# One listed order for every engine, one PSUM pool of eight banks, and denominators in PSUM, in a three-layer kernel

## The chip, the cores and the metric

The kernel runs on one core of one Trainium2 chip. The metric is the device time of one launch in microseconds; the median of the runs is compared. Engines go by their names in the profile: PE is TensorE, PEld its weight loads, DVE VectorE, ACT ScalarE, POOL GpSimd, and SP the queue that issues every transfer of this kernel.

## What is computed

The program is a gated linear recurrence (an mLSTM), followed by two MLPs on its outputs.

```python
for t in range(S):                                  # B, H, S, D = 2, 8, 768, 40
    m_new = np.maximum(f_gate[:, :, t] + m, i_gate[:, :, t])
    f_stab = np.exp(f_gate[:, :, t] + m - m_new)
    i_stab = np.exp(i_gate[:, :, t] - m_new)
    C = f_stab * C + i_stab * outer(vt, kt)         # state, 40 x 40 per head
    n = f_stab * n + i_stab * kt
    denom = np.maximum(np.abs(n . qt), 1.0)
    y[:, :, t] = sigmoid(o_gate[:, :, t]) * (C @ qt) / denom
x = y, as 1536 tokens x 320
x = ((x @ w_a) * (x @ w_b)) @ w_out                 # d_ff = 1536
g = x @ w_in                                        # d_ff = 2048
return (g * sigmoid(g)) @ w_out2
```

## The kernel before

**Units.** The recurrence is computed in chunks of 128 steps. A unit u is one chunk of one batch (12 units; u's chunk is u // 2). `load_q`, `load_k`, `load_kvo` and `load_fs` fetch a unit's data. `scores` makes q k products (`s_u`), `weigh` multiplies them by the decay matrix `e_u`, which `decays` makes on VectorE, `values` multiplies by v (`y_u`, from L360), `carried` adds what the state brings (`y_u`, from L370), `update` and `advance` make the next state. `combine` and `outputs` give the unit's x, and `x_transposed` turns it and splits it into a high and a low part in `xring`. Units 0 and 1 have no state before them; their decays come from `factors` (`fb_u`), those of later units from a table in DRAM (`fsd`).

**First MLP.** Its 12 weight blocks of 128 hidden columns arrive as 64-bit numbers. `split_w1` narrows each one on ScalarE and VectorE and splits it into a high and a low part (ScalarE copies, GpSimd subtracts at L195). The tail rows are moved to other partitions by a transfer (`w_j` from `tl_j`). `PASSES` cuts the work into passes: a block of 2 or 3 units against 5, 3, 4 or all 12 weight blocks. In a pass, a step `m3.5.a` is the first product of pass 3 with weight block 5, `.b` the second one with the multiply (L526) and the split of g, `.c` the second layer into accumulators, and `.end` writes x1, with one evicting instruction for all columns and one more for the 64 tail columns. The pass products are TensorE line 479, the second layer lines 488 to 490.

**Second MLP.** It goes in three blocks of 4 units against 16 weight blocks, in a loop behind the list (`prep2`, `block`, `slots`).

**What sets the order.** The steps are written down in `ORDER`, and a scheduler places each instruction on its engine from there: steps with `!` get a higher priority, `AFTER` holds back three steps, and 150 warm-up matmuls (`warm`) have the lowest priority of all, so that they fill gaps. The second MLP is not in the list. SP issues transfers in the order that the scheduler gives. PSUM has three pools: 3 banks of accumulators, 2 for first-layer products (and the scores of units 0 to 3), 3 for everything else of the recurrence.

**Denominators.** In `outputs` VectorE makes max(-y, y) (L426), max with 1 (L428) and the reciprocal (L429) in SBUF, multiplies (L431) and copies the last 64 columns of x once more behind it (L434), for the transposes.

## Time and profile before

| | |
|---|---|
| median of 3 runs | 492.58 us (492.13 to 498.36) |
| span of the profiled execution | 524.2 us |
| that execution's own time around the span | not on the page |
| TensorE busy in it | 506.7 us (97%) |
| VectorE, ScalarE, GpSimd busy | 197.0, 206.7, 254.8 us |
| mean granted clock of TensorE | 0.828 |

Durations of single instructions come from the one profiled execution. A busy time of TensorE counts matmuls that overlap and modelled ends, so it tells when the engine has something in it and not how fast it goes. The granted clock is a share of 2.4 GHz; the profile shows two values here, 0.85 and 0.50 (1.2 GHz), and a stretch's value is the mean of them.

### The profile page before, as it was taken

Reading aid. Unit: us, or ns where it says so; the run is one execution under the profiler, and the core shown is the slowest. Engines: PE = TensorE matmul, PEld = TensorE weight load, DVE = VectorE, ACT = ScalarE, POOL = GpSimd, SP = SyncE. Lnnn points to the kernel's source line nnn. Section 1 sums busy time; section 2 is a strip of 40 time slices with the busy share of each in tenths; the row PEclk is TensorE's granted clock in tenths of the full one; section 3 lists DMA queues with packets and bytes.
Section 4 is the critical chain, followed back from the end, with each engine's and each line's share of the span. In section 5 each row is a group of like instructions: output and inputs, shape, how many; then the busy total and the mean of one; then the engine's idle time right before and its main releaser. Section 6 shows DMA issues by size and latency. Waiting matters only on the chain.

```text
span 524.2 us, 8077 instructions
## 1 busy us (share of the span) xinstructions
PE 506.7 (97%) x3133; PEld 478.7 (91%) x3133; DVE 197.0 (38%) x328; ACT 206.7 (39%) x447; POOL 254.8 (49%) x289
## 2 busy tenths in 40 slices
PE   7999989699999999999999999999999999999996
PEld 6999879699999999999999999888888888889885
DVE  7677988968433345423731545300000000000000
ACT  4235665553222321212744545833334332342322
POOL 5429897896532241313753687843332233232331
PEclk9576887868888888888888888888888888888888
DMA  6475875734310011301450344000001000010001
GB/s 231 155 226 159 257 218 170 242 98 113 92 57 1 1 60 61 94 1 55 135 197 1 111 157 137 38 1 1 1 0 51 0 1 1 0 51 0 2 0 50
DMA packets 25089, 42.30 MB, mean 81 GB/s; under 512 B 2156, under 2 KB 18348, under 8 KB 25052
## 3 DMA queue, kind: packets, MB, share of 16 engines
q1 hardware_dynamic: 25052, 41.80, 25.5%
q8 instruction: 24, 0.39, 0.3%
q14 instruction: 13, 0.11, 0.1%
HBM read 38.99 MB, written 2.02 MB: 78 GB/s over the span
## 4 chain that ended last, share of the span: by engine, by line
PE 79%; POOL 8%; DVE 4%; ACT 4%; DMA 2%; issue 2%; SPq 0%; ACTq 0%; POOLq 0%; DVEq 0%
PE h L479 38%; PE acc L488 9%; PE acc L489 9%; PE acc L490 9%; POOL w_j L195 5%; PE s_u L347 5%; PE y_u L360 3%; PE warm L298 2%; ACT cvt_j L188 2%; PE px_u L458 1%; POOL g L195 1%; PE y_u L370 1%; DVE e_u L327 1%; PE fb_u L318 1%; POOL tl_j L195 1%
## 5 line engine op out<-in xcount | busy, mean ns | idle before, releaser
L479 PE MATMUL h<-xring,w_j 128*128 128x256 f32 (+2 forms) x1088 | 202.6, 333 | 3.5 <-DVE g L526 2.5
L479 PEld LDWEIGHTS h<-xring,w_j 128*128 128x128 f32 x1088 | 174.0, 198 | 9.9 <-DVE g L526 3.3
L195 POOL TENSOR_TENSOR g2w<-gw,g2w 128x512 fp32r<-128x512 f32 x48 | 61.7, 1287 | 117.6 <-ACT g2w L499 117.6
L195 POOL TENSOR_TENSOR g<-g,g 128x256 fp32r<-128x256 f32 (+1 forms) x60 | 54.7, 911 | 92.0 <-ACT g L499 91.8
L195 POOL TENSOR_TENSOR w_j<-cvt_j,w_j 128x320 fp32r<-128x320 f32 (+2 forms) x72 | 68.7, 955 | 6.6 <-ACT w_j L223 3.0
L479 PE MATMUL h<-xeven,w_j 128*128 128x512 f32 x256 | 71.0, 417 | 0.2 <-ACT gw L531 0.2
L531 ACT ACTIVATE gw<-h 128x512 f32<-128x512 f32 x48 | 28.8, 600 | 87.4 <-PE h L479 84.0
L488 PE MATMUL acc<-w_j,g2w 128*128 128x320 f32 x192 | 61.1, 324 | 0.0
L489 PE MATMUL acc<-w_j,g2w 128*128 128x320 f32 x192 | 60.9, 323 | 0.0
L479 PEld LDWEIGHTS h<-xeven,w_j 128*128 128x128 f32 x256 | 48.1, 192 | 11.6 <-ACT gw L531 0.5
L499 ACT CAST g<-g 128x256 fp32r<-128x256 f32 (+1 forms) x60 | 26.8, 447 | 71.7 <-DVE g L526 71.6
L526 DVE TENSOR_TENSOR g<-a,h 128x256 f32<-128x256 f32 (+1 forms) x60 | 28.1, 469 | 65.0 <-PE h L479 58.5
L488 PE MATMUL acc<-w_j,g 128*128 128x320 f32 x144 | 47.1, 331 | 0.0
L489 PE MATMUL acc<-w_j,g 128*128 128x320 f32 x144 | 46.1, 324 | 0.0
L520 ACT ACTIVATE a<-h 128x256 f32<-128x256 f32 (+1 forms) x60 | 25.6, 426 | 50.4 <-PE h L479 50.4
L190 DVE SCALAR_TENSOR_TENSOR cvt_j<-raw_j,cvt_j 128x704 uint32<-128x704 uint32 (+2 forms) x40 | 42.9, 1074 | 0.9
L490 PE MATMUL acc<-w_j,g2w 128*128 128x320 f32 x192 | 41.3, 323 | 0.0
L499 ACT CAST g2w<-gw 128x512 fp32r<-128x512 f32 x48 | 29.8, 621 | 28.0 <-PE acc L490 27.2
L488 PEld LDWEIGHTS acc<-w_j,g2w 128*128 128x128 f32 x192 | 36.9, 192 | 2.4
L489 PEld LDWEIGHTS acc<-w_j,g2w 128*128 128x128 f32 x192 | 36.7, 191 | 2.4
L188 ACT ACTIVATE cvt_j<-raw_j 128x704 f32<-128x704 f32 (+2 forms) x40 | 28.8, 724 | 23.4 <-POOL w_j L195 21.3
L490 PE MATMUL acc<-w_j,g 128*128 128x320 f32 x144 | 36.5, 328 | 0.7 <-POOL g L195 0.7
(95 smaller groups left out, 642.3 us busy)
## 6 DMA issues: line engine op xcount, KB each, us to landing
raw_j<-in_w_dram SPq DMA_DIRECT2D x16, 704.0 KB, 5.4
raw_j<-in_w_dram SPq DMA_DIRECT2D x12, 512.0 KB
kvo_u<-in_kvo_dram SPq DMA_DIRECT2D x12, 480.0 KB, 3.8
raw_j<-in_w_dram SPq DMA_DIRECT2D x12, 448.0 KB, 5.1
e_u<-fsd SPq DMA_DIRECT2D x10, 512.0 KB
qT_u<-in_q_cols_dram SPq DMA_DIRECT2D x12, 180.0 KB, 3.1
kz<-in_k_cols_dram SPq DMA_DIRECT2D x36, 60.0 KB
out_dram<-osb SPq DMA_DIRECT2D x12, 160.0 KB, 1.8
```

Source lines behind the costliest of these rows:

```text
L188: nc.scalar.activation(out=c, in_=hi32.bitcast(F32), func=ACT.Prelu, scale=2.0 ** -111, alpha=-2.0 ** 32)
L190: nc.vector.scalar_tensor_tensor(out=cu, in0=lo32, scalar=29, in1=cu, op0=ALU.logical_shift_right, op1=ALU.bitwise_or)
L195: return eng.tensor_tensor(out=out_, in0=x, in1=hi.bitcast(F32), op=ALU.subtract)
L347: nc.tensor.matmul(out=s[:, i], lhsT=kz[u % 2][:, j, g], rhs=un["q", u][:, g], start=True, stop=True)
L479: nc.tensor.matmul(out=po, lhsT=w[:, wi * P:(wi + 1) * P], rhs=xt[:, :, xi], start=(n == 0), stop=(n == len(pairs) - 1))
L488: nc.tensor.matmul(out=o, lhsT=hi, rhs=w[:, off:off + DM], start=first, stop=False)
L489: nc.tensor.matmul(out=o, lhsT=hi, rhs=w[:, off + DM:off + 2 * DM], start=False, stop=False)
L490: nc.tensor.matmul(out=o, lhsT=lo, rhs=w[:, off:off + DM], start=False, stop=last)
L499: nc.scalar.copy(out=t[:, 0], in_=g)
L520: nc.scalar.activation(out=a[j], in_=pa, func=ACT.Copy, scale=WS ** -2)
L526: nc.vector.tensor_tensor(out=g, in0=a.pop(j), in1=pb, op=ALU.mult)
L531: nc.scalar.activation(out=g, in_=ph, func=ACT.Silu, scale=1 / WS)
```

## The change

The list grows to 1,535 steps, each a single operation on a single engine (but for a few set-up steps), and every engine issues in the listed order (`tc.manual_schedule()`), with no priorities. The second MLP, its weight splits (`x3.p` ...) and its transposes (`y4.px` ...) are in the list too. The 150 warm-up matmuls become steps of four; `FILL` defines 90 such groups and the list places 30 of them. All of PSUM is one pool of 8 banks. The denominators are made in a PSUM bank: ScalarE takes the absolute value into it, VectorE clips and inverts it there. ScalarE makes the copies of the 64 tail columns, and the small copy of the input gate into `vx_u`, which was GpSimd's. The factor products read 128 partitions in place of 16.

```diff
-zeros li l0.q l0.k lf l1.k l1.q l0.t const warm run0 expi0 bmask l1.t pg0 run1 expf0 expf1 expi1 u0.f0 !u0.s0
...
+li const zeros lf run0 f9 f13 f1 f22 f4 lw0.b lw0.a w0.bp w0.bs f28 f25 f24 l1.t l0.t expi0 w0.bo w0.hb w0.t0 pg0
...
-AFTER = {'w1.a': 'u1.out', 'w1.b': 'u1.out', 'u4.d0': 'u3.w1'}
...
-    WARM = 150
+    FILL = 90
...
-    ps_acc = ctx.enter_context(tc.tile_pool(name="ps_acc", bufs=3, space=PSUM))
-    ps_ab = ctx.enter_context(tc.tile_pool(name="ps_ab", bufs=2, space=PSUM))
+    ps = ctx.enter_context(tc.tile_pool(name="ps", bufs=8, space=PSUM))
...
-    ps_at = att_ctx.enter_context(tc.tile_pool(name="ps_at", bufs=3, space=PSUM))
+    def bank(name, *shape):
+        return ps.tile(list(shape), F32, tag="b", name=name)
...
     def warm(n):
-        p = ps_acc.tile([P, P], F32, tag="acc", name="warm")
-        with tc.high_priority(-3000):
-            for _ in range(n):
-                nc.tensor.matmul(out=p, lhsT=idb, rhs=idb, start=True, stop=True)
+        if "warm" not in un:
+            un["warm"] = bank("warm", P, P)
+        for _ in range(n):
+            nc.tensor.matmul(out=un["warm"], lhsT=idb, rhs=idb, start=True, stop=True)
...
-                nc.tensor.matmul(out=f[:, i], lhsT=ident[0:BH, r:r + 1].to_broadcast([BH, P]),
-                                 rhs=fs[:, s_], start=True, stop=True)
+                nc.tensor.matmul(out=f[:, i], lhsT=ident[:, r:r + 1].to_broadcast([P, P]),
+                                 rhs=scratch[1][:, s_], start=True, stop=True)
...
-            nc.gpsimd.tensor_copy(out=vx[:, :, D:DV], in_=isb.unsqueeze(2))
+        def scale_i():
+            nc.scalar.copy(out=v_tile()[:, :, D:DV], in_=isb.unsqueeze(2))
...
-            dn = at.tile([P, H, 1], F32, tag="dn", name=f"dn_u{u}")
-            nc.vector.scalar_tensor_tensor(out=dn, in0=y[:, :, D:DV], scalar=-1.0, in1=y[:, :, D:DV],
-                                           op0=ALU.mult, op1=ALU.max)
-            nc.vector.tensor_scalar(out=dn, in0=dn, scalar1=1.0, scalar2=None, op0=ALU.max)
-            nc.vector.reciprocal(out=dn, in_=dn)
+        def magnitudes():
+            T["dn"] = bank(f"dn_u{u}", P, H, 1)
+            nc.scalar.activation(out=T["dn"], in_=T["y"][:, :, D:DV], func=ACT.Abs)
+
+        def denominators():
+            nc.vector.tensor_scalar(out=T["dn"], in0=T["dn"], scalar1=1.0, scalar2=None, op0=ALU.max)
+
+        def inverses():
+            nc.vector.reciprocal(out=T["dn"], in_=T["dn"])
...
-            return nc.vector.tensor_copy(out=x[:, DM:3 * P], in_=x[:, 2 * P:DM])
...
+    def x_tail(x):
+        nc.scalar.copy(out=x[:, DM:3 * P], in_=x[:, 2 * P:DM])
...
-                for lo, to in ((0, 0), (2 * P, DM)):
-                    d = x1[u][:, to:to + DM - lo]
...
+            d = x1[u][:, 0:DM]
...
+    with tc.manual_schedule():
+        for t in ORDER:
+            parts[t]()
```

Three places show how the instructions stand. On TensorE, around the first product of the first MLP, before (`w_j_426` and `w_j_519` are weight blocks 0 and 1, `s_u`, `y_u` and `ups_u` belong to units 2 and 3):

```order
L479 MATMUL h<-xring,w_j_426 128x256 x5
L347 MATMUL s_u_548<-qT_u_396,kz_108 128x128 x4
L289 MATMUL pgb<-scratch 120x6 x6
L479 MATMUL h<-xring,w_j_426 128x256 x3
L360 MATMUL y_u_623<-vx_u_538,e_u_466 128x41 x4
L347 MATMUL s_u_554<-qT_u_396,kz_108 128x128 x4
L370 MATMUL y_u_636<-cn_u_533,qT_u_396 128x123 x2
L370 MATMUL y_u_636<-cn_u_533,qT_u_396 128x82
L380 MATMUL ups_u_660<-vx_u_538,kvo_u_446 120x123 x3
L479 MATMUL h<-xring,w_j_426 128x256 x8
L360 MATMUL y_u_623<-vx_u_538,e_u_466 128x41
```

and in the change, from the last fillers of the early part on (`w_j_174`, `w_j_391` and `w_j_365` are blocks 0, 2 and 1, `s_u` and `y_u` are unit 3's):

```order
L404 LDWEIGHTS idb
L404 MATMUL warm<-idb 128x128
L622 MATMUL h<-xring,w_j_174 128x256 x8
L622 MATMUL h<-xring,w_j_391 128x256 x8
L457 MATMUL s_u_616<-qT_u_471,kz_103 128x128 x4
L622 MATMUL h<-xring,w_j_174 128x256 x8
L457 MATMUL s_u_634<-qT_u_471,kz_103 128x128 x4
L622 MATMUL h<-xring,w_j_391 128x256 x8
L622 MATMUL h<-xring,w_j_365 128x256 x16
L470 MATMUL y_u_675<-vx_u_462,e_u_552 128x41 x8
L631 MATMUL acc<-w_j_174,g_688 128x320
L632 MATMUL acc<-w_j_174,g_688 128x320
```

Before, the first block's two products stood with recurrence work of units 2 and 3 between them. Now six products of three blocks stand together, ahead of block 0's second layer.

On SP, around the load of unit 2's k, v and o, before (`kvo_u_446` is unit 2's and `kvo_u_478` unit 3's, `w_j_426` takes the tail moves of block 0):

```order
L151 DMA kz_109<-in_k_cols_dram 40x384 x2
L214 DMA w_j_426<-tl_j_431 64x128
L172 DMA raw_j_593<-in_w_dram 128x896
L162 DMA e_u_480<-fsd 128x8x128
L156 DMA kvo_u_446<-in_kvo_dram 128x960
L172 DMA raw_j_595<-in_w_dram 128x1024
L156 DMA kvo_u_478<-in_kvo_dram 128x960
L214 DMA w_j_519<-tl_j_524 64x128 x2
L172 DMA raw_j_597<-in_w_dram 128x896
```

and in the change (`kvo_u_518` is unit 2's, `w_j_391` and `w_j_365` take the tail moves of blocks 2 and 1, `raw_j_547` and `raw_j_555` are block 3):

```order
L229 DMA raw_j_337<-in_w_dram 128x896
L199 DMA qT_u_339<-in_q_cols_dram 120x384
L220 DMA e_u_464<-fsd 128x8x128
L199 DMA qT_u_471<-in_q_cols_dram 120x384
L209 DMA kz_102<-in_k_cols_dram 40x384 x3
L214 DMA kvo_u_518<-in_kvo_dram 128x960
L229 DMA raw_j_547<-in_w_dram 128x896
L293 DMA w_j_391<-tl_j_427 64x128
L220 DMA e_u_552<-fsd 128x8x128
L293 DMA w_j_365<-tl_j_367 64x128
L229 DMA raw_j_555<-in_w_dram 128x1024
L293 DMA w_j_365<-tl_j_367 64x128
```

Before, both loads of e stood ahead of unit 2's load, and now e of unit 3, block 3 and the tail moves of two blocks stand behind it; that load waits for the buffer that unit 0 leaves.

On VectorE, at the outputs of unit 1 (`dn_u`, `x_u`) and the low part of its transposed x (the second `xring` row), before:

```order
L426 SCALAR_TENSOR_TENSOR dn_u_459<-y_u_452 128x8
L428 TENSOR_SCALAR dn_u_459<-dn_u_459 128x8
L429 RECIPROCAL dn_u_459<-dn_u_459 128x8
L195 TENSOR_TENSOR xring<-px_u_418,xring 128x384
L431 TENSOR_TENSOR x_u_463<-kvo_u_299,dn_u_459 128x320
L434 COPY x_u_463<-x_u_463 128x64
```

and in the change (`cvt_j_473` is the narrowing of block 1, `e_u_464` belongs to unit 2):

```order
L549 TENSOR_SCALAR dn_u_439<-dn_u_439 128x8
L255 SCALAR_TENSOR_TENSOR cvt_j_473<-raw_j_246,cvt_j_473 128x512
L552 RECIPROCAL dn_u_439<-dn_u_439 128x8
L464 TENSOR_TENSOR e_u_464<-s_u_484,e_u_464 128x512
L556 TENSOR_TENSOR x_u_531<-kvo_u_168,dn_u_439 128x320
L260 TENSOR_TENSOR xring<-px_u_476,xring 128x384
L464 TENSOR_TENSOR e_u_464<-s_u_493,e_u_464 128x512
L535 TENSOR_TENSOR y_u_535<-y_u_511,isg 128x328
L260 TENSOR_TENSOR xring<-px_u_538,xring 128x384
```

The negate-and-max and the copy of the tail are gone from this engine. The low part of unit 1's x was VectorE's 47th row after its opening branch, twelve behind the first row shown of before, and is the last row shown of the change, its 50th.

## Rows read from the trace of the kernel before

**Rows 1.** The page's first line.

```profile
span 524.2 us, 8077 instructions
```

**Rows 2.** Busy time by stretch: length, engines' busy us (instructions), granted clock, DMA share, GB/s.

```profile
0.00:43.00 43.00, 38.62 (x306) 37.00 (x307) 31.01 (x50) 15.94 (x34) 19.84 (x45) 0.74 0.63 201
43.00:117.00 74.00, 65.69 (x431) 63.22 (x431) 62.97 (x92) 42.59 (x111) 66.46 (x72) 0.75 0.64 194
117.00:519.60 402.60, 402.37 (x2399) 378.44 (x2398) 103.05 (x187) 147.21 (x302) 168.49 (x174) 0.85 0.15 46
519.60:524.20 4.60, 0.00 (x0) 0.00 (x0) 0.00 (x0) 0.99 (x4) 0.00 (x0) 0.84 0.40 143
```

**Rows 3.** TensorE's groups of instructions, 0 to 117 us: count, busy us, mean ns, idle before.

```profile
L479 PE MATMUL h<-xring,w_j 128*128 128x256 f32 x184 | 31.6, 314 | 3.5 <-DVE g L526 2.5 <-POOL w_j L195 0.5 <-ACT a L520 0.4
L347 PE MATMUL s_u<-qT_u,kz 120*128 120x128 f32 x113 | 23.7, 370 | 0.0
L360 PE MATMUL y_u<-vx_u,e_u 128*128 128x41 f32 x98 | 16.8, 314 | 0.7 <-DVE e_u L354 0.7
L298 PE MATMUL warm<-idb 128*128 128x128 bf16 x150 | 14.7, 274 | 3.5 <-DVE idb L564 3.5
L488 PE MATMUL acc<-w_j,g 128*128 128x320 f32 x20 | 6.9, 351 | 0.0
L489 PE MATMUL acc<-w_j,g 128*128 128x320 f32 x20 | 6.6, 335 | 0.0
L380 PE MATMUL ups_u<-vx_u,kvo_u 128*120 128x123 f32 x36 | 6.3, 310 | 0.0
L318 PE MATMUL fb_u<-scratch,ident 16*128 16x128 f32 x32 | 6.2, 357 | 0.0
L458 PE MATMUL px_u<-ident,x_u 128*128 128x128 f32 x18 | 5.0, 314 | 3.4 <-DVE x_u L431 3.2 <-DVE x_u L434 0.2
L370 PE MATMUL y_u<-cn_u,qT_u 120*128 120x123 f32 (+1 forms) x24 | 4.9, 342 | 0.0
L490 PE MATMUL acc<-w_j,g 128*128 128x320 f32 x18 | 4.7, 336 | 0.7 <-POOL g L195 0.7
```

**Rows 4.** The chain of waits, 140 to 160 us: start us, us, what, how many.

```profile
144.47 1.99 PE h L479 x16
...
146.47 0.16 PE acc L488
...
147.42 1.01 PE s_u L347 x8
...
151.38 1.88 PE y_u L360 x16
```

**Rows 5.** The timeline of VectorE, then of TensorE, 0 to 60 and 0 to 130 us.

```profile
40.58 0.54 DVE L195 TENSOR_TENSOR xring<-px_u,xring 128x384 fp32r<-128x384 f32 x1
...
42.19 0.64 PE L479 MATMUL h<-xring,w_j 128*128 128x256 f32 x3
```

**Rows 6.** The chain of waits, 0 to 125 us.

```profile
31.66 5.37 DMA e_u<-fsd
...
68.98 2.14 POOL vx_u L332
...
96.52 5.17 DMA qT_u<-in_q_cols_dram
```

**Rows 7.** Groups by form over the span: count, busy us, mean ns.

```profile
L426 DVE SCALAR_TENSOR_TENSOR dn_u<-y_u 128x8 f32<-128x8 f32 x12 | 5.3, 439 | 1.4 <-ACT y_u L416 1.2
...
L434 DVE COPY x_u<-x_u 128x64 f32<-128x64 f32 x12 | 5.1, 427 | 0.3
...
L548 ACT ACTIVATE x<-acc 128x64 f32<-128x64 f32 x12 | 2.8, 236 | 0.0
```

**Rows 8.** GpSimd's groups by form, 0 to 117 us: a block's 512 columns split.

```profile
L195 POOL TENSOR_TENSOR w_j<-cvt_j,w_j 128x512 fp32r<-128x512 f32 x11 | 14.9, 1355 | 0.1
```

More of the change, by code (lines that the diff above doesn't have):

```diff
@@ L342, in scores @@
         def scores(n):
-            pool, tag = (ps_ab, "ab") if early else (ps_at, "at")
-            s = pool.tile([P, 4, C], F32, tag=tag, name=f"s_u{u}")
+            s = bank(f"s_u{u}", P, 4, C)
             for i in range(4):
@@ L444, in tile_mlstm_gated_mlps @@
+        return d
     px = {}
@@ L552, in mlp, with evict, two, gate @@
-        return {"a": one, "b": two, "c": three, "end": end}
+            A["p", j] = first_layer(W[1, j], PAIRS[1, 0], x_columns(m, blk), nt)
+        def evict(j):
+            A[j] = hidden(m, "a")[:, 0:nt]
+            nc.scalar.activation(out=A[j], in_=A.pop(("p", j)), func=ACT.Copy, scale=WS ** -2)
+        def two(j):
+            PB[j] = first_layer(W[m, j], PAIRS[m, m % 2], x_columns(m, blk), nt)
+        def gate(j):
+            Q[j] = hidden(m, "g")[:, 0:nt]
+            if m == 1:
+                nc.vector.tensor_tensor(out=Q[j], in0=A.pop(j), in1=PB.pop(j), op=ALU.mult)
+            else:
+                nc.scalar.activation(out=Q[j], in_=PB.pop(j), func=ACT.Silu, scale=1 / WS)
@@ new lines, in high, with low, three, end @@
+        def high(j):
+            G2[j] = hidden(m, "g2", 2)[:, :, 0:nt]
+            nc.scalar.copy(out=G2[j][:, 0], in_=Q[j])
+        def low(j):
+            rest(nc.gpsimd, G2[j][:, 1], Q.pop(j), G2[j][:, 0])
+        def three(j):
+            if not acc:
+                acc.extend(bank("acc", P, 512) for _ in units)
+            left.remove(j)
+            second_layer(acc, G2.pop(j), W[m, j], off, len(left) == len(js) - 1, not left)
+        def end(n):
+            u, y = units[n], acc[n]
+            if m == 2:
+                b, c, s = place(u)
+                o = P2["wp2"].tile([P, DM], F32, tag="osb", name="osb", bufs=4)
+                nc.scalar.activation(out=o, in_=y[:, 0:DM], func=ACT.Copy, scale=1 / WS)
+                nc.sync.dma_start(out=out[b * S + c * C:b * S + (c + 1) * C, :], in_=o)
+                return
+            d = x1[u][:, 0:DM]
+            if js[0] == 0:
+                nc.scalar.activation(out=d, in_=y[:, 0:DM], func=ACT.Copy, scale=1 / WS)
+            else:
+                nc.vector.scalar_tensor_tensor(out=d, in0=y[:, 0:DM], scalar=1 / WS, in1=d,
+                                               op0=ALU.mult, op1=ALU.add)
@@ L555, in tile_mlstm_gated_mlps @@
+        f = dict(b=two, g=gate, h=high, l=low, c=three)
+        if m == 1:
+            f.update(a=one, e=evict)
+        return f, {f"z{n}": lambda n=n: end(n) for n in range(len(units))}
     ch = [chunk(u) for u in range(NT)]
@@ L659, in tile_mlstm_gated_mlps @@
[L659 to L668 removed]
+        for x in range(2):
+            parts[f"lw{j}.{'ab'[x]}"] = lambda j=j, x=x: load_w1(j, x)
+        parts.update({f"w{j}.{n}": f for n, f in split_w1(j).items()})
@@ L672 @@
+    for n, m, blk, js in stages:
+        each, ends = mlp(m, blk, js)
+        for j in js:
+            parts.update({f"{n}.{j}.{x}": lambda f=f, j=j: f(j) for x, f in each.items()})
+        parts.update({f"{n}.{x}": f for x, f in ends.items()})
+    with tc.manual_schedule():
+        for t in ORDER:
+            parts[t]()
 _OUTS = [((1536, 320), "float32")]
```

503 lines of the change are left out of this document (265 added, 238 removed).

## The prediction

> **What bounds the kernel now.** I read the span first [rows 1], then four stretches of it [rows 2]. From 117.0 to 519.6 us TensorE is busy for 402.4 of 402.6 us at a granted clock of 0.85, while VectorE, ScalarE and GpSimd are busy for 103, 147 and 169 us. Nothing but TensorE's own work sets that stretch, and the change takes no matmul out of it. The last 4.6 us are the four output evictions and their store. So what an order can win lies before 117 us, and I count how much of that time TensorE needs.
>
> [Rows 3] count the matmul passes before 117 us. What one costs at full speed is read from the dense stretch, as the step from one to the next [rows 4]: 1.99 us for 16 products of 256 columns (0.125), 1.01 for 8 scores (0.126), 1.88 for 16 value products (0.1175), 0.16 for a second-layer matmul of 320 columns. The means in rows 3 overlap each other and aren't used. The sum: 184 x 0.125 = 23.0; scores 113 x 0.126 = 14.2; values 98 x 0.1175 = 11.5; second layer 58 x 0.157 = 9.1 (0.157, from 320 columns at the 256-column rate of 2.04 a ns); updates 36 and carried products 24 at the values' 0.1175 = 7.0; factor rows 32 and transposes 18 at the scores' 0.126 = 6.3; small gate products some 2.2. That is 73.3 us. The first 117 us thus hold 73.3 us of needed work and 43.7 us of waiting, warm-up matmuls (150) and work at the slow clock.
>
> The 43.7 us fall into two parts. Until x of units 0 and 1 is ready, TensorE can't begin the first layer; VectorE writes the last piece of it at 40.58 to 41.12 us, and the first product is whole at 42.8 us [rows 5]. From 43 to 117 us TensorE has some 55 us of work and takes 74. About 7 of the lost 19 us are clock: at a mean of 0.75 [rows 2], 55 us of work at 0.85 takes 62. The rest are waits; VectorE is busy for 63.0 us of the 74 and GpSimd for 66.5, and the chain of waits in it goes over GpSimd's and VectorE's pieces and transfers [rows 6]. So that stretch is bound by the helpers, and one reason is that 11 of the 12 weight blocks are split before 117 us [rows 8], though the passes that run then use only blocks 0 to 4.
>
> **What the change does to each part.**
>
> *The start, until the first product.* Every engine now follows the list, and the last VectorE instruction on the path to x of unit 1 is its 50th; before it was its 47th (the order piece of VectorE). Before, VectorE needed 31.0 us for 50 instructions in the first 43 us [rows 2], so 12 us of it were idle. Ahead of that instruction the list has now put the splits of blocks 0, 1 and 2 whole; adding up my rows' durations for the 50 gives 34.5 us, some 4.5 more than the 47 held. If the idle time takes it all in, x is ready at 41; if none, at 46. To this comes the transfer order: SP now issues unit 2's k, v and o ahead of three other loads and of the moves of block 2's tails (the order piece of SP), and that load waits until unit 0's output multiply has read o. I take 44 us for the first product's start, with 40 (two of the idle gaps closed) and 52 (the extra work and one exposed transfer of 5.2 to 5.4 us [rows 6] after 41) as ends. Thirty groups of 4 fillers replace 150 warm-up matmuls; they stand where TensorE would otherwise wait, so I count their change at nothing, except through the clock (a rival below).
>
> *From the first product to the end of the early work.* Ahead of the first product the new list puts 22.9 us of needed TensorE work: 48 score passes x 0.126, 48 values x 0.1175, 32 factor rows x 0.126, 18 updates and 12 carried products x 0.1175, 12 transposes x 0.126, gates 2.2. So 73.3 - 22.9 = 50.4 us are left to reach the point that was reached at 117 us. What do the helpers have to do beside that? Up to the same amount of TensorE work the list gives VectorE 61 instructions and GpSimd 43. At the means of the stretch before (62.97/92 = 0.68 us and 66.46/72 = 0.92 us [rows 2]) that is 42 and 40 us, under the 50.4. They fall because blocks 8 to 11 are mostly split later, beside the dense stretch, where these engines were idle for 60% and more. TensorE becomes the bound here. Products of several blocks are put back to back before the first second-layer group (the order piece of TensorE: between block 0's second product and its second layer stand a score group, three products and unit 3's values, 1.0 + 3.0 + 1.9 = 5.9 us), which covers the eviction, multiply and split of g. I put 5 us of waits on this stretch: 1 if the list meets them as it means to, 19 if as much is lost as now.
>
> *The dense stretch.* 402.6 us of work remain. A fixed order can only lose here; I take 2 us, ends 0 and 8. *The end* stays at 4.6 us.
>
> *Denominators, copies and PSUM.* The negate-and-max (0.44 us mean) and the tail copy (0.43) leave VectorE, 12 each; ScalarE gets 12 absolute values and the tail copies, for which its 64-column copy from PSUM at 0.24 us is the nearest row [rows 7]. Twelve times 0.87 us off VectorE is 10.4 us, about half of it before 117 us, but VectorE is no longer the bound by my count, and ScalarE has 74 - 42.6 = 31 us free there [rows 2]. I price this at 0 on the path; 0.24 us more to 0.6 less for each of units 0 and 1, whose outputs are on the path of the start. The small copies into v move from GpSimd, where one of them stood in the chain with 2.14 us [rows 6], to ScalarE. One pool of 8 banks in place of 3, 2 and 3 lets up to four products wait for their eviction; its cost is a wait only if a bank is asked for too early, which the 5 us hold.
>
> *Sum against the profiled execution:* 44 + 50.4 + 5 + 402.6 + 2 + 4.6 = 508.6 us for a span of 524.2, so 15.6 us less. The span is 31.6 us longer than the median of the runs, 492.58; what lies around it isn't on the page. If the start takes the same in both, the saving is 15.6 us; in proportion (492.58/524.2 = 0.94) it is 14.7. I take 15.6: 477.0 us. The ends of the terms give 40 + 50.4 + 1 + 402.6 + 0 + 4.6 = 498.6 and 52 + 50.4 + 19 + 402.6 + 8 + 4.6 = 536.6.
>
> **Rivals.**
>
> *The start gets longer and eats the gain.* VectorE has more to do ahead of x, and the loads of weights now stand ahead of q and k. With the first product at 52 us the sum is 516.6, hence 485.0. For it: VectorE's 31.0 busy us in 43 already. Against: 12 idle us there.
>
> *The clock.* In the first 43 us the granted clock was 0.74 and from 43 to 117 us 0.75 [rows 2], so TensorE fell to its 1.2 GHz level for a part of both. There are fewer fillers now, in groups of 4 with work between. If the 22.9 us of work ahead of the first product ran at 0.50 all along, they would take 22.9 x 0.85 x (1/0.50 - 1/0.74) = 12.6 us longer; with half of that on the path, and the next 50.4 us at 0.75 again (6.7 us), the sum is 521.6 and the time 490.0, no change that can be told. The Trainium skill has a rule that speaks for this ("TensorE: Matmul & The Clock Gate", the section "A second HAM failure mode: psum-queue depth-cycling"): a kernel that goes round the PSUM banks makes TensorE pause shortly between groups and so lets its clock swing. The trace of before doesn't agree where it is dense: 117 to 519.6 us hold 0.85 with the two first-layer banks in turn, though no run yet shows eight in one pool. By that rule the dense stretch would not stay at 0.85.
>
> *One transfer holds up a whole queue (the slower side).* SP issues in one listed order, and each load or tail move that has to wait for a buffer holds all behind it. e of a unit took 5.37 us and q 5.17 on the chain [rows 6]. If for each of units 2 to 5 one of these lands in full view, 4 x 5.3 = 21 us are added, with the start at 52 us 29 in all: 537.6, hence 506.0. It decides for slower once the new order loses over 25.4 us more than my sum (508.6 to 534.0, 2% over the span's share of 492.58). Against: q of units 2 and 3 and e of unit 2 are issued before the load that waits, and the transfers were busy for 0.63 of the time, not full.
>
> *How the numbers follow.* The forecast case 0.68: of it 0.64 ends under 482.7 us, 0.04 above. A longer start 0.13 (0.05 still faster by over 2%, 0.08 within). The clock 0.09, within 2%. The held queue 0.10, slower. So faster by over 2% is 0.69, within 2% 0.21, slower 0.10; 2% is about what a measurement of this kernel can tell from no change, as its three runs lie 1.3% apart. The range has to leave out no more than 0.2: 467 (the low end of the terms, 25.6 us less) to 492, which holds the longer start and the clock case and leaves out the held queue.
>
> **What would show it.** Right: the first whole product near 44 us; TensorE within some 5 us of full from there to the end; 73.3 us of work done by about 100 us and not 117; VectorE and GpSimd at under 85% from 44 to 100 us, and busy for longer after that; clock 0.85 from the first product on. Wrong at the start: VectorE's 50th instruction after 48 us, with SP waiting ahead of unit 2's loads. Wrong on the clock: slices at 0.50 after the first product. Wrong on the bound: TensorE waiting in sum for over 20 us after the first product, on GpSimd's splits or on transfers.

## The result, and the profile after

The change takes 476.18 us (median of 4 runs, 475.0 to 476.78) against 495.47 us for the kernel before in the same session (4 runs, 492.13 to 498.84): a ratio of 0.9598, 95% interval 0.953 to 0.9666. The forecast was 477.0 us and faster.

The profiled execution of before on which the prediction rests had TensorE at 0.85 in its dense stretch; the change's ran at 1.00 there. Durations of the two can't be compared one by one, so the kernel before was run again; that execution took 497.28 us, and its rows stand beside those of the change. It is one of the slower ones of that kernel, with a mean granted clock of 0.970, where five of seven others in its session took 492.06 to 493.37 us at 0.972 to 0.983, so the 22.2 us between the two profiles are some 3 us more than the 19.3 between the medians. Its span, then its windows (columns as in [rows 2]):

```profile
span 495.5 us, 8077 instructions
...
0.00:39.00 39.00, 35.15 (x288) 33.63 (x288) 27.82 (x45) 14.15 (x30) 16.45 (x39) 0.78 0.65 210
39.00:65.00 26.00, 22.53 (x171) 21.86 (x172) 24.10 (x39) 16.66 (x42) 24.64 (x30) 0.93 0.68 219
65.00:91.00 26.00, 20.48 (x150) 19.21 (x149) 22.62 (x32) 14.59 (x41) 23.63 (x25) 0.93 0.63 200
91.00:117.00 26.00, 23.08 (x175) 22.42 (x175) 22.02 (x33) 16.12 (x42) 23.63 (x28) 0.94 0.55 165
117.00:200.00 83.00, 81.78 (x659) 81.31 (x658) 40.61 (x85) 22.08 (x59) 33.86 (x43) 1.00 0.19 57
200.00:491.00 291.00, 289.24 (x1698) 270.15 (x1697) 60.98 (x98) 121.31 (x234) 133.53 (x127) 1.00 0.14 47
```

The change, answering [rows 1, 2]:

```profile
span 473.3 us, 7980 instructions
...
0.00:39.00 39.00, 34.02 (x300) 32.59 (x301) 32.91 (x51) 18.64 (x48) 24.42 (x42) 0.96 0.69 218
39.00:65.00 26.00, 22.63 (x172) 21.75 (x172) 24.54 (x32) 13.58 (x41) 17.25 (x19) 0.93 0.69 226
65.00:91.00 26.00, 25.48 (x208) 24.89 (x207) 20.89 (x35) 17.63 (x51) 20.91 (x26) 1.00 0.52 167
91.00:117.00 26.00, 26.00 (x210) 25.96 (x209) 10.50 (x17) 13.82 (x38) 16.78 (x27) 1.00 0.51 141
117.00:200.00 83.00, 82.55 (x635) 82.29 (x634) 36.72 (x71) 25.24 (x72) 38.00 (x41) 1.00 0.20 60
200.00:468.70 268.70, 268.14 (x1585) 250.94 (x1584) 55.55 (x89) 116.31 (x234) 126.45 (x125) 1.00 0.16 53
```

Busy TensorE time doesn't tell how much is done, so I priced every matmul but the fillers with its step in a stretch at full clock. The change's chain of waits shows such steps, answering [rows 4]: 0.120 us per 256-column product, 0.112 per score.

```profile
140.15 1.92 PE h L622 x16
...
149.92 1.79 PE s_u L457 x16
```

Needed work done, us at full clock (an estimate: what each matmul would take by these steps, added up by stretch):

| stretch, us | before (again) | change | scheduler (e3) | early splits (e6) |
|---|---|---|---|---|
| 0 to 39 | 14.8 | 20.0 | 12.7 | 19.0 |
| 39 to 65 | 19.8 | 19.8 | 16.6 | 16.2 |
| 65 to 91 | 17.3 | 24.7 | 23.3 | 10.7 |
| 91 to 117 | 20.8 | 25.8 | 15.6 | 13.7 |
| by 117 | 72.8 | 90.3 | 68.1 | 59.6 |
| in all | 440.9 | 439.6 | 440.5 | 439.9 |

The spans differ by 22.2 us. By this sum 5.2 us of it were won before 39 us, nothing from 39 to 65, 12.3 from 65 to 117, and the other 4.7 behind that. The groups of TensorE up to 117 us say the same without a price: the change had done 335 first-layer products, before 199 (184 in [rows 3]).

```profile
L622 PE MATMUL h<-xring,w_j 128*128 128x256 f32 x335 | 45.8, 290 | 1.2 <-DMA w_j<-tl_j 0.9
L457 PE MATMUL s_u<-qT_u,kz 120*128 120x128 f32 x96 | 13.8, 293 | 0.1
L470 PE MATMUL y_u<-vx_u,e_u 128*128 128x41 f32 x96 | 11.6, 279 | 2.3 <-issue 2.2
```

From 65 to 117 us TensorE's longest waits in the kernel before were these (waiter, releaser: sum, times, longest), with 8.3 us in all; in the change one of 0.4 us is left.

```profile
PE h L479 <- DVE g L526: 3.1, 2, 2.7
PE px_u L458 <- DVE x_u L431: 2.8, 1, 2.8
PE acc L490 <- POOL g L195: 0.8, 1, 0.8
PE h L479 <- POOL w_j L195: 0.6, 1, 0.6
```

Half clock costs as much as the work that falls into it (in the change a 256-column product took 0.24 us at 0.50, 0.120 at 1.00). Before, the clock stood at 0.50 from 12.0 to 29.1, 42.7 to 46.2 and 87.1 to 93.9 us, with 10.3 us of needed work; in the change from 28.9 to 32.3 and 52.8 to 56.2, with 3.4 (the record begins at 8.6 us before and at 11.9 in the change, and the steps ahead of that are slow in both). So, as an estimate, 7 of the 22.2 us are clock that no longer fell, 1.3 are work that ran at a slightly shorter step (0.227 in place of 0.230 us for 512 columns), and the rest, some 14 us, is waiting and fillers. The 7 are a high end: the mean clock was 0.976 over seven runs of before and 0.988 over four of the change, about half the distance of these two profiles (0.970 and 0.992). The change's two windows at half clock, called cold below:

```profile
28.90:32.30 3.40, 3.40 (x22) 3.33 (x20) 2.72 (x4) 1.32 (x7) 3.12 (x3) 0.50 0.79 269
52.80:56.20 3.40, 3.40 (x18) 3.40 (x17) 3.40 (x3) 2.20 (x8) 3.40 (x5) 0.50 0.67 215
```

The start in the timelines of VectorE and TensorE, answering [rows 5]: unit 1's low part at 38.17 us (40.05 in the second profile of before, the last two rows), the first product at 39.19, with its eight matmuls through at 40.4 (42.1).

```profile
38.17 0.54 DVE L260 TENSOR_TENSOR xring<-px_u,xring 128x384 fp32r<-128x384 f32 x1
...
39.19 1.43 PE L622 MATMUL h<-xring,w_j 128*128 128x256 f32 x10
...
40.05 0.54 DVE L195 TENSOR_TENSOR xring<-px_u,xring 128x384 fp32r<-128x384 f32 x1
...
41.52 0.62 PE L479 MATMUL h<-xring,w_j 128*128 128x256 f32 x3
```

By form, answering [rows 7, 8]: ScalarE's tail copy and absolute value, VectorE's clip, and GpSimd's 512-column splits up to 117 us (9, where before had 11).

```profile
L596 ACT COPY x_u<-x_u 128x64 f32<-128x64 f32 x12 | 2.8, 244 | 5.0 <-DVE x_u L556 5.0
L546 ACT ACTIVATE dn_u<-y_u 128x8 f32<-128x8 f32 x12 | 2.1, 182 | 13.9 <-DVE y_u L539 12.9 <-DVE e_u L464 1.0
L549 DVE TENSOR_SCALAR dn_u<-dn_u 128x8 f32<-128x8 f32 x12 | 2.0, 164 | 1.3 <-ACT dn_u L546 1.3
...
L260 POOL TENSOR_TENSOR w_j<-cvt_j,w_j 128x512 fp32r<-128x512 f32 x9 | 13.6, 1512 | 5.8 <-ACT w_j L272 5.6
```

### The profile page after: what moved, and what is told of

It is laid out like the page before. It is cut to its first block, busy times and chain, and to the rows that moved or that the text cites. A ratio compares the mean times of both kernels' runs of the same rounds, so it can differ in the third digit from the quotient of the medians.

```text
span 473.3 us, 7980 instructions
## 1 busy us (share of the span) xinstructions
PE 460.0 (97%) x3103; PEld 439.3 (93%) x3103; DVE 181.1 (38%) x292; ACT 206.8 (44%) x483; POOL 243.8 (52%) x278
## 4 chain that ended last, share of the span: by engine, by line
PE 80%; DVE 3%; POOL 2%; ACT 1%; issue 1%; POOLq 0%; DVEq 0%
PE h L622 43%; PE acc L633 10%; PE acc L631 10%; PE acc L632 10%; PE s_u L457 2%; PE y_u L470 2%; DVE cvt_j L255 1%; PE px_u L593 1%; POOL g L260 1%; PE ups_u L490 1%; PE y_u L480 1%; DVE cvt_j L251 1%; POOL w_j L260 0%; ACT w_j L283 0%; DVE g L661 0%
## 5 line engine op out<-in xcount | busy, mean ns | idle before, releaser
L622 PE MATMUL h<-xring,w_j 128*128 128x256 f32 (+2 forms) x1088 | 180.4, 317 | 1.2 <-DMA w_j<-tl_j 0.9
L622 PEld LDWEIGHTS h<-xring,w_j 128*128 128x128 f32 x1088 | 163.2, 191 | 6.4 <-DMA w_j<-tl_j 1.1
L260 POOL TENSOR_TENSOR g<-g,g 128x256 fp32r<-128x256 f32 (+1 forms) x60 | 61.4, 1029 | 54.1 <-ACT g L667 51.8
L260 POOL TENSOR_TENSOR w_j<-cvt_j,w_j 128x320 fp32r<-128x320 f32 (+3 forms) x72 | 62.6, 876 | 42.3 <-ACT w_j L321 18.9
L622 PE MATMUL h<-xeven,w_j 128*128 128x512 f32 x256 | 62.4, 392 | 0.0
L633 PE MATMUL acc<-w_j,g2w 128*128 128x320 f32 x192 | 59.8, 311 | 0.1
L631 PE MATMUL acc<-w_j,g2w 128*128 128x320 f32 x192 | 59.5, 310 | 0.0
L632 PE MATMUL acc<-w_j,g2w 128*128 128x320 f32 x192 | 59.3, 309 | 0.0
L631 PE MATMUL acc<-w_j,g 128*128 128x320 f32 x144 | 46.2, 321 | 0.1
L633 PE MATMUL acc<-w_j,g 128*128 128x320 f32 x144 | 44.9, 312 | 1.3 <-POOL g L260 1.3
L632 PE MATMUL acc<-w_j,g 128*128 128x320 f32 x144 | 44.5, 309 | 0.0
L251 DVE TENSOR_SCALAR cvt_j<-cvt_j 128x704 uint32<-128x704 uint32 (+2 forms) x40 | 29.2, 731 | 38.3 <-ACT cvt_j L246 38.2
L631 PEld LDWEIGHTS acc<-w_j,g2w 128*128 128x128 f32 x192 | 36.1, 188 | 1.0
L632 PEld LDWEIGHTS acc<-w_j,g2w 128*128 128x128 f32 x192 | 36.1, 188 | 1.0
L633 PEld LDWEIGHTS acc<-w_j,g2w 128*128 128x128 f32 x192 | 36.0, 188 | 0.8 <-POOL g2w L260 0.6
```

Of the source, the lines that this page charges most:

```text
L251: nc.vector.tensor_scalar(out=cu, in0=cu, scalar1=3, scalar2=None, op0=ALU.logical_shift_left)
L260: return eng.tensor_tensor(out=out_, in0=x, in1=hi.bitcast(F32), op=ALU.subtract)
L622: nc.tensor.matmul(out=po, lhsT=w[:, wi * P:(wi + 1) * P], rhs=xt[:, :, xi], start=(n == 0), stop=(n == len(pairs) - 1))
L631: nc.tensor.matmul(out=o, lhsT=hi, rhs=w[:, off:off + DM], start=first, stop=False)
L632: nc.tensor.matmul(out=o, lhsT=hi, rhs=w[:, off + DM:off + 2 * DM], start=False, stop=False)
L633: nc.tensor.matmul(out=o, lhsT=lo, rhs=w[:, off:off + DM], start=False, stop=last)
```

## The experiments

Ratios are to the kernel before on the same chip, whose medians were 493.0 to 495.5 us. The change's own session has the highest, 495.47, so its 0.9598 is up to 0.005 lower than it would be beside the lowest; where a ratio and the medians disagree below, that is a part of the reason. A profile also gives the lag of the same TensorE instruction behind the change's profile, which is finer than the times, but one execution of the change scatters too: the runs below are 1.2 to 3.6 us late before 28 us already, mostly through single waits for early loads and splits. I read the lag from there on, except for e1, whose missing fillers stand in that part.

| lag in us at the change's | 27.4 (`pgb`) | 39.2 (first product) | 53.3 | 63.7 | end |
|---|---|---|---|---|---|
| e1 no fillers | 3.6 | 3.5 | 6.0 | 4.7 | 4.5 |
| e2 both on VectorE | 1.2 | 3.5 | 5.7 | 4.4 | 6.8 |
| e4 clip in SBUF | 1.3 | 1.4 | 3.8 | 2.4 | 3.0 |
| e5 tails on VectorE | 1.5 | 5.2 | 2.6 | 2.7 | 3.0 |
| e7 shift moved | 1.2 | 2.4 | 0.4 | 1.5 | 1.5 |
| e9 shift from PSUM | 3.3 | 3.3 | 2.7 | 2.4 | 2.5 |
| e11 port order | 2.8 | 2.8 | -0.8 | 1.7 | 1.7 |

**e0: the kernel before, unchanged.** 

> The kernel before, unchanged, for a profile whose clock can be set beside the change's (0.992 granted there, 0.828 in the profile that the prediction was read from). All theories: the needed TensorE work is the same 440 us as in the change at that clock, so a span of 490 to 497 us holds 50 to 57 us of loss against 34 in the change. The theory that the early stretch is where the time went expects the first whole product at 41 to 43 us (39 to 42 in the change) and 25 to 35 us lost behind it (10 in the change). The theory that an earlier start gave the time expects the first product after 50 us.

497.28 us; its profile is the one above. The first whole product came at 42.1 us, as the theory of the early stretch has it, and not after 50.

**e3: the scheduler places the change's steps.**

```diff
-    with tc.manual_schedule():
-        for t in ORDER:
-            parts[t]()
+    for t in ORDER:
+        parts[t]()
```

> The change's steps in the same list and with the same pool of 8 banks, but placed by the scheduler as before, not issued in the listed order. My theory (the listed order, by which the helpers do early only what is needed early, is the gain): 484 to 500 us, VectorE and GpSimd over 85% busy behind the first product. The rival that the single pool of banks and the smaller steps gave the gain: 474 to 480 us.

503.82 us, ratio 1.0212 (1.0169 to 1.0254): slower than before and beyond my 484 to 500, and some 28 us slower than the change, with the same single pool, denominators, copies, steps and fillers. TensorE's longest waits are for `e_u` (5.0 us), the last outputs (4.3) and g (2.5), the first product begins at 51.3 us, the clock stood at 0.50 for 37.5 us in three stretches, and at 117 us 68.1 us of work are done. Behind the first product VectorE was over 85% busy (23.8 of 26 us from 39 to 65), GpSimd was not (17.8). So without the fixed order the rest of the change gains nothing. Two limits: the scheduler got the list without the priorities and the `AFTER` holds that it had before, so some of the loss against before may be theirs; and no run puts the three pools, the narrower factor products or GpSimd's small gate copy back under the fixed order, so what these are worth in it stays open.

**e1: the 30 filler groups left out.**

```diff
-li const zeros lf run0 f9 f13 f1 f22 f4 lw0.b lw0.a w0.bp w0.bs f28 f25 f24 l1.t l0.t ...
+li const zeros lf run0 lw0.b lw0.a w0.bp w0.bs l1.t l0.t ...
```

> The change without its 30 groups of fillers; the rest of the list as it is. If the fillers only fill waits and the clock does not depend on them: 475 to 478 us. If the clock of the start hangs on them: TensorE at 1.2 GHz for most of the first 39 us, the first product 4 to 8 us later and 480 to 485 us.

478.78 us, ratio 0.9706 (0.9653 to 0.976), 2.6 us more than the change by the medians and 5 by the ratios, whose intervals overlap; that lies between the two forecasts. The trace shows the mechanism: TensorE's factor products ran at half speed until 19.9 us, where the change's were quick from 11.9 us on. Without fillers (timeline of TensorE):

```profile
17.18 1.92 PE L423 MATMUL fb_u<-scratch,ident 128*128 128x128 f32 x8
```

and in the change:

```profile
16.86 1.16 PE L423 MATMUL fb_u<-scratch,ident 128*128 128x128 f32 x8
```

The cold stretches are 26.7 to 30.1, 33.6 to 40.4 and 54.0 to 60.9 us, 17 us in place of 6.8. The traces of e4, e5, e7, e9 and e11, with all fillers, have 3.4 to 13.7 us of it, and their record of full clock begins at 6.3 to 11.9 us, so it is the late first rise, at 19.9 us, that stands out. Fillers where TensorE waits pay for the clock of the work behind them; it is a small part of the gain.

**e2: denominators and tail copies on VectorE, in SBUF, in the listed order.**

```diff
-            T["dn"] = bank(f"dn_u{u}", P, H, 1)
-            nc.scalar.activation(out=T["dn"], in_=T["y"][:, :, D:DV], func=ACT.Abs)
+            T["dn"] = at.tile([P, H, 1], F32, tag="dn", name=f"dn_u{u}")
+            nc.vector.scalar_tensor_tensor(out=T["dn"], in0=T["y"][:, :, D:DV], scalar=-1.0, in1=T["y"][:, :, D:DV],
+                                           op0=ALU.mult, op1=ALU.max)
...
-        nc.scalar.copy(out=x[:, DM:3 * P], in_=x[:, 2 * P:DM])
+        nc.vector.tensor_copy(out=x[:, DM:3 * P], in_=x[:, 2 * P:DM])
```

> The change with the denominators in SBUF as before (negate-and-max on VectorE) and the tail copies on VectorE, the order as it is. My theory (VectorE is not the bound behind the start; the moves are worth nothing on the path): 476 to 479 us, at most 1 us for each of units 0 and 1 at the start. The rival that the moves off VectorE gave the gain: 483 to 490 us.

481.59 us, ratio 0.9757 (0.9715 to 0.9798), clear of the change's interval. All four of its runs (480.28 to 481.81) lie above all of the change's. My price of 0 fell, and the time lies between the two forecasts. Two runs take up a part each; the absolute value itself on VectorE stands in neither.

**e4: the absolute value by ScalarE, but into SBUF.**

```diff
-            T["dn"] = bank(f"dn_u{u}", P, H, 1)
+            T["dn"] = at.tile([P, H, 1], F32, tag="dn", name=f"dn_u{u}")
```

> The change with one edit: ScalarE still takes the absolute value, VectorE still clips and inverts, but in a tile in SBUF and not in a PSUM bank. My theory: in SBUF the clip lasts until the row of instructions that GpSimd is in has ended (0.17 us where GpSimd is idle, up to 1.2 us where it is not, as in the kernel before), in PSUM 0.12 to 0.17 us always. So the 12 clips take a mean of 0.45 us or more, and the time is 477 to 480 us, 1 to 4 above the change. Rival: the place makes no difference and the gain comes from taking the absolute value off VectorE: clips at 0.17 us and 475.5 to 476.5 us.

478.97 us, ratio 0.9667 (0.9613 to 0.9722). The clip of 8 numbers a partition takes 535 ns in place of 164 (by form):

```profile
L549 DVE TENSOR_SCALAR dn_u<-dn_u 128x8 f32<-128x8 f32 x12 | 6.4, 535 | 1.4 <-ACT dn_u L546 1.4
```

In SBUF the clip waits for the GpSimd instruction that it meets. In the kernel before run again, 9 of 12 clips ended 25 to 30 ns behind the end of the GpSimd instruction that was running when they began, and took 0.36 to 1.22 us; the other three, with GpSimd idle, took 0.16 to 0.17. GpSimd's row of instructions may go on behind: the clip at 63.97 us ended with the first of two (VectorE, then GpSimd).

```profile
63.97 0.78 DVE L428 TENSOR_SCALAR dn_u<-dn_u 128x8 f32<-128x8 f32 x1
...
63.44 1.28 POOL L424 TENSOR_TENSOR kvo_u<-kvo_u,y_u 128x320 f32<-128x320 f32 x1
64.68 1.27 POOL L195 TENSOR_TENSOR w_j<-cvt_j,w_j 128x512 fp32r<-128x512 f32 x1
```

So my theory, that the clip lasts until the whole row has ended, asked for too much, though the mean and the time came as forecast. The Trainium skill has this ("SBUF — State Buffer", section "Who interferes with whom"): VectorE and GpSimd share a pair of SBUF ports, which VectorE's copies and scalar operations from SBUF to SBUF can take whole, and who comes second is blocked. The trace agrees, with 164 ns from PSUM, beside a busy GpSimd in 9 of 12 cases, and up to 1.22 us from SBUF.

**e5: the tail copies by VectorE.**

```diff
-        nc.scalar.copy(out=x[:, DM:3 * P], in_=x[:, 2 * P:DM])
+        nc.vector.tensor_copy(out=x[:, DM:3 * P], in_=x[:, 2 * P:DM])
```

> The change with one edit: VectorE makes the copies of the 64 tail columns again (all of them, those of x1 for the second MLP too), at the place in the list where ScalarE makes them. My theory: the copy of unit 1 stands on VectorE behind a decay product and behind GpSimd's row, so the transposes of unit 1 and the first product come some 2 us later (41 us in place of 39.2): 477.5 to 480 us. Rival: the denominators alone make the 5.4 us that both edits together cost, and this one gives 475.5 to 477.

478.76 us, ratio 0.9659 (0.9594 to 0.9725). TensorE waits 3.6 us in two transposes (table of waits, 34 to 60 us):

```profile
PE px_u L593 <- DVE x_u L596: 3.6, 2, 1.9
```

because unit 1's copy stands behind a decay product and another multiply on VectorE, at 39.59 us. In the lag the 5.2 us at the first product are down to 2.6 at 53.3. Neither e4 nor e5 alone is clear of the change's interval; e2, which has both and the absolute value too, is. By the medians they lose 2.8, 2.6 and 5.4 us.

**e10: the denominators of the change in the kernel before.**

```diff
-            dn = at.tile([P, H, 1], F32, tag="dn", name=f"dn_u{u}")
-            nc.vector.scalar_tensor_tensor(out=dn, in0=y[:, :, D:DV], scalar=-1.0, in1=y[:, :, D:DV],
-                                           op0=ALU.mult, op1=ALU.max)
+            dn = ps_at.tile([P, H, 1], F32, tag="at", name=f"dn_u{u}")
+            nc.scalar.activation(out=dn, in_=y[:, :, D:DV], func=ACT.Abs)
```

> The kernel before, its scheduler and its pools kept, with the denominators alone done as in the change: ScalarE takes the absolute value into a PSUM bank of the recurrence's pool, VectorE clips and inverts there. My theory: the 12 clips fall from a mean of 0.57 us to 0.12 to 0.17, and 12 negate-and-max of 0.44 us leave VectorE, some 4 us of it before 117 us where it binds: 488 to 492 us. Rival: the third bank of that pool is then missing elsewhere, or the scheduler orders the rest another way: 493 to 498 us.

494.11 us, ratio 0.9976 (0.9944 to 1.0008). The clips fell to 165 ns as expected, and the time didn't follow: under the scheduler this edit is worth at most 0.6%. As e4's 0.7% isn't clear of noise either, the two don't show that the order decides what the place in PSUM is worth, and the bank that this edit takes from a pool of three isn't tested by itself.

**e8: the kernel before with four blocks' splits taken off the helpers (VectorE and GpSimd).** It leaves out the low halves of these blocks; ScalarE copies in GpSimd's place.

```diff
+        if light:
+            return c
         nc.vector.tensor_scalar(out=cu, in0=cu, scalar1=3, scalar2=None, op0=ALU.logical_shift_left)
...
+        light = j >= 8
+
+        def rest_(out_, x, hi):
+            if light:
+                nc.scalar.copy(out=out_, in_=x)
+            else:
+                rest(nc.gpsimd, out_, x, hi)
```

> The kernel before with the work of VectorE and GpSimd on weight blocks 8 to 11 taken out: their low halves are not merged (no shift, no merge on VectorE) and ScalarE copies where GpSimd subtracted, so those four blocks carry wrong weights. Loads, tail moves and TensorE's work stay. Some 2.1 us of VectorE and 3.1 to 4 us of GpSimd a block go, most of it before 117 us. My theory: the load of these two engines binds that stretch in the kernel before, so 5 to 12 us of the time go: 481 to 489 us. Rival: single waits in a chain (queues, transfers, eviction) bind it, and less load on engines that wait anyway gives 0 to 3 us: 490 to 494 us.

489.64 us, ratio 0.9912 (0.9868 to 0.9955): 4.4 us of 495, between the two forecasts. Up to 117 us VectorE and GpSimd were busy for 91.0 and 82.5 us, 5.6 and 5.9 less than in before run again; the change takes 7.7 and 9.0 off them. So the helpers' load counts, but some two thirds of that relief bring only a quarter of what the change brings.

**e6: the splits of blocks 4 to 11 earlier in the list.**

```diff
-... u3.si l2.e u2.d0 f3 l3.q ... lw11.b (step 363) ... w11.v1 (step 695)
+... each such step behind 263 at 263 + 0.55 x (step - 263)
```

> The change with the loads and splits of the weight blocks behind step 263 of the list (blocks 4 to 11) moved forward, each to 55% of its distance from that step, their order among themselves kept. Nothing else moves. My theory: the early part is quick because these splits are put off until VectorE and GpSimd are idle; with four more blocks in it (some 2.1 us of VectorE and 3.1 us of GpSimd each) these two are over 85% busy again between 39 and 117 us, TensorE waits for them, and the time is 480 to 488 us. Rival: where the splits stand is of no account, what counts is that every engine has a fixed order at all: 475 to 478 us.

508.22 us, ratio 1.0259 (1.0184 to 1.0334), beyond both forecasts and not for my reason: from 65 to 91 us every engine is idler than in the change, not busier.

```profile
65.00:91.00 26.00, 14.87 (x87) 14.70 (x88) 11.66 (x17) 8.51 (x22) 12.51 (x17) 0.70 0.41 128
```

TensorE waits in single long stops (39 to 117 us):

```profile
PE s_u L455 <- DMA w_j<-tl_j: 7.3, 1, 7.3
PE y_u L478 <- POOL cn_u L522: 6.4, 2, 5.0
PE acc L631 <- POOL g L258: 6.3, 1, 6.3
```

Tail moves and loads now stand in SP's queue ahead of unit loads, and splits ahead of state updates, and each holds what is behind it. 8.2 us of TensorE's waits end with a transfer, which is the mechanism of my third rival; 12.7 us end with GpSimd's `cn_u` and g, and GpSimd itself stood 4.0 us until 87.7 us for a load of k, v and o. The clock stood at 0.50 for 37.5 us, so a part of the loss is its. An order that only moved weights (and one tail move of block 3) did this. It leaves untested what the deferral is worth in load alone.

**e7: block 4's shift behind unit 3's decay products.** In the change TensorE waits 2.2 us at 48 us for unit 3's `e_u`, and VectorE's shift ahead of it lasts 3.46 us; it ends 0.25 us behind GpSimd's row, five instructions back to back (one of 0.46 us ran when the shift began). Most shifts wait for less: the one at 70.51 us took 0.92, until 0.25 us behind the one GpSimd instruction that it met, while the row went on. Why some wait for the whole row isn't shown. VectorE:

```profile
45.54 3.46 DVE L251 TENSOR_SCALAR cvt_j<-cvt_j 128x448 uint32<-128x448 uint32 x1 [0.21 <-ACT cvt_j L246]
49.03 0.62 DVE L255 SCALAR_TENSOR_TENSOR cvt_j<-raw_j,cvt_j 128x448 uint32<-128x448 uint32 x1
49.58 1.28 DVE L464 TENSOR_TENSOR e_u<-s_u,e_u 128x512 f32<-128x512 f32 x2
```

and GpSimd meanwhile, back to back:

```profile
45.88 0.73 POOL L450 TENSOR_TENSOR kvo_u<-kvo_u,e_u 128x320 f32<-128x320 f32 x1
46.58 0.72 POOL L444 TENSOR_TENSOR vx_u<-kvo_u,isg 128x320 f32<-128x320 f32 x1
47.26 0.73 POOL L260 TENSOR_TENSOR g<-g,g 128x256 fp32r<-128x256 f32 x1
47.96 0.79 POOL L542 TENSOR_TENSOR kvo_u<-kvo_u,y_u 128x320 f32<-128x320 f32 x1
```

```diff
-... w4.bp w4.bs w4.bo u3.sk u3.sv u3.w0 u3.v0 u3.w1 u3.v1
+... w4.bp u3.sk u3.sv u3.w0 u3.v0 u3.w1 w4.bs w4.bo u3.v1
```

> The change with two steps moved: the shift and the merge of weight block 4's first half on VectorE (the shift took 3.46 us at 45.5 us, until GpSimd's row ended) go behind unit 3's two decay products, which TensorE's 2.2 us of idle time at 48 us wait for. My theory: that wait goes, 473 to 475 us, and if the half clock from 52.8 to 56.2 us was its consequence 1.7 us more, 471.5 to 473.5 us. Rival: another wait takes its place (the eviction and multiply of the next block, or block 4 itself), 475 to 477 us.

476.25 us, ratio 0.9607 (0.9545 to 0.9669): no difference from the change. The wait went from 2.2 to 0.4 us, and the clock stayed at 1.00 from 39.2 us on; the lag fell from 2.4 to 0.4 us at the change's 53.3. By 63.7 it was 1.5 again: the other half of block 4 took 3.88 us on VectorE in the same way, and unit 3's transposes waited 1.4 us behind it. The rival held.

**e9: the shift reads PSUM.**

```diff
-            T["c"] = c()
+            if key[:2] in VIA:
+                T["c"] = bank("via_j%d" % key[1], P, n)
...
-            nc.vector.tensor_scalar(out=cu, in0=cu, scalar1=3, scalar2=None, op0=ALU.logical_shift_left)
+            nc.vector.tensor_scalar(out=cu, in0=src, scalar1=3, scalar2=None, op0=ALU.logical_shift_left)
```

> The change with one edit: for weight block 4 ScalarE writes the narrowed numbers into a PSUM bank, and VectorE's shift reads them there and writes SBUF, so that it doesn't wait for GpSimd. In the change these two shifts took 3.46 and 3.83 us at 45.5 and 53.1 us, and TensorE waited 2.2 us for the decay products behind the first. My theory: both take 0.5 to 0.8 us, VectorE gets some 6 us back between 39 and 65 us, TensorE's wait goes, and the time is 471 to 474.5 us. Rival: as when the shift was moved, the next wait takes its place within 20 us, and the time stays at 475 to 477 us.

476.33 us, ratio 0.9636 (0.9593 to 0.9679): again no difference. The shifts took 0.62 and 0.69 us, and the merge behind them, with two inputs from SBUF, took over the wait (VectorE):

```profile
49.15 0.62 DVE L260 TENSOR_SCALAR cvt_j<-via_j 128x448 uint32<-128x448 uint32 x1 [0.31 <-ACT via_j L252]
49.81 2.72 DVE L264 SCALAR_TENSOR_TENSOR cvt_j<-raw_j,cvt_j 128x448 uint32<-128x448 uint32 x1
...
56.68 3.33 DVE L264 SCALAR_TENSOR_TENSOR cvt_j<-raw_j,cvt_j 128x512 uint32<-128x512 uint32 x1
```

**e11: eight steps moved to keep the two apart.**

```diff
-w3.ha w3.la ... w4.bs w4.bo ... m0.0.l ... w4.t1 w4.u1 ... u2.ox ... w4.as w4.ao ... w4.ha u3.rc u3.ox
+w3.ha ... m0.0.l w3.la ... u2.ox w4.bs w4.bo w4.t1 w4.u1 ... u3.rc u3.ox w4.as w4.ao w4.ha
```

> The change with eight steps moved so that VectorE's shifts and merges don't meet GpSimd's rows ahead of something TensorE waits for: GpSimd's low part of weight block 3 goes behind unit 3's two scalings and the split of g; VectorE's shift and merge of block 4's first half, with a tail split and its move, go behind unit 2's outputs; the shift, merge and copy of its second half go behind unit 3's outputs. My theory: the decay products of unit 3 come some 3 us earlier, TensorE's 2.2 us wait ahead of them goes, and with it the half clock from 52.8 to 56.2 us (1.7 us): from the first product to the end 430 to 432.5 us in place of 434.1, and 472 to 474.5 us in all. Rival: VectorE and GpSimd have no time left over there, and the wait comes back at block 4 or at unit 3's transposes within 20 us, as it did when the shift alone was moved: 433 to 435 us behind the first product, 475 to 478 in all.

476.6 us, ratio 0.9661 (0.9592 to 0.9731). From the first product to the end it took 433.0 us, as the rival has it. The lag shows how: from 2.8 us at the first product to -0.8 at 53.3, the 3.6 us I wanted, and then 2.5 lost at once. ScalarE stood 3.2 us before a copy that waits for block 4's merge, which I had put off, and the tail copy of unit 2 behind it came late (ScalarE, then TensorE):

```profile
52.97 0.30 ACT L281 CAST w_j<-cvt_j 64x128 fp32r<-64x128 f32 x1 [3.20 <-DVE cvt_j L253]
...
55.66 0.25 ACT L594 COPY x_u<-x_u 128x64 f32<-128x64 f32 x1
...
55.96 0.33 PE L591 MATMUL px_u<-ident,x_u 128*128 128x128 f32 x1 [2.13 <-ACT x_u L594]
```

No run here beats the change.

## Why the prediction was right, step by step

**What bounds the kernel.** Right where it mattered: TensorE's work was the floor, and what an order can win lay mostly before 117 us, 17.5 of 22.2 us by the table.

**The sum** came closer than its terms. The saving was put at 15.6 us and was 19.3 by the medians and 22.2 between the profiles. The time is nevertheless within 0.8 us of 477.0, because the kernel before, 492.58 us when the forecast was made, has 495.47 with a fourth run. That is luck. Between the profiles the early part gave the 17.6 us that were forecast, and the whole difference of 6.6 us lies behind it, where I had put a loss of 2 us and 4.6 were won.

**The start** was put at 44 us and came at 39.2, below its low end of 40, and whole at 40.4. VectorE did have more to do (51 instructions and 32.9 us up to 39 us, 45 and 27.8 before), and the idle time took it all in; my 44, which lets three fifths of it show, was too careful. The transfer order cost little there: TensorE's one wait for a transfer, a tail move in the middle of its first products, is 0.9 us.

**The early work.** I put the point that before reached at 117 us at 44 + 50.4 + 5 = 99.4 us. By the table's prices the change had done before's 72.8 us at 99.4 us. That is luck in part: the start was 4.8 us early, and from there on it took 60.2 us for 52.8 us of work, so 7.4 were lost where I put 5 and the work was 2.4 more. And the profile of e10, with before's list and scheduler and no different in time from before, has that work done at about 113 us, so some 4 of the 17.6 us may belong to the one execution of before that stands beside the change. From 91 us on TensorE had no gap, as said; from 39 to 65 us it did no more than before, with VectorE busy for 24.5 of 26 us. From 44 to 100 us VectorE and GpSimd were busy for 78% and 73%, under the 85% that I had as a sign. The clock fell once behind the first product, for 3.4 us.

**The reason I gave for the helpers' load** holds at equal work, and its size was off. When the change had done before's 72.8 us, at 99.4 us, 7 of 12 blocks' 512-column pieces were split, and VectorE and GpSimd had been busy for 81.2 and 68.6 us; before took 11 pieces and 96.6 and 88.4 us for that work. From the first product to there they had 71 and 55 instructions of 48.1 and 44.2 us, where I had counted 61 and 43 of 42 and 40. But less load is the smaller part of the gain: e8 has 4.4 us for some two thirds of the change's relief up to 117 us. That the larger part is the order itself, which keeps each engine from standing before work that another needs, is argued and not measured by itself; shown is that with the scheduler (e3) nothing is left of the gain, and that another listed order (e6) turns it into a loss.

**Denominators and copies** were priced at 0 on the path, with 0.6 us less for each of units 0 and 1 as the far end. This term was mis-sized: e2 puts it at 5.4 us by the medians (nearly 8 by the ratios, of which 2.5 are the distance of before's medians in the two sessions). Two things were missed. The row of the clip was not read: its mean of 573 ns for eight numbers, beside 198 for the reciprocal of the same eight, stood in the trace of before and says that something else is in it (by form).

```profile
L428 DVE TENSOR_SCALAR dn_u<-dn_u 128x8 f32<-128x8 f32 x12 | 6.9, 573 | 0.2
L429 DVE RECIPROCAL dn_u<-dn_u 128x8 f32<-128x8 f32 x12 | 2.4, 198 | 0.3
```

And the copy's place in a fixed order was not read: on VectorE it stands behind work of the next unit. A saving on an engine that "is no longer the bound" is not free when its instruction stands on the path.

**The dense stretch** was put at 2 us longer, as "a fixed order can only lose here", and that step failed: from the 99.4 us point to the end the change took 373.9 us, before 378.5 from 117. Before left gaps of 3.0 us behind 117 us outside the last 4.5 us, the change 1.0, and the 512-column steps were a little shorter. **The end**, from the last matmul on, was 4.6 us before and 3.5 in the change, whose first output eviction starts at 468.56 us with matmuls running until 469.84.

**Rivals.** The longer start didn't come. The clock didn't fall for good: it stood at 1.00 from 56.2 to 472.7 us, behind the last matmul, with eight banks in one pool. The Trainium skill's rule that going round the PSUM banks lets the clock swing ("TensorE: Matmul & The Clock Gate", section "A second HAM failure mode: psum-queue depth-cycling") isn't what this trace shows. The held queue didn't come in the change. In e6 it did, but its 32 us mix it with splits ahead of state updates and with half clock, so my 21 us for four transfers stay unchecked.
